# Block-diagonal states, one product per head pair, a flipped Gram copy by DMA, and a newly planned order, in a delta-rule attention with a GELU feed-forward

## The chip, the cores and the metric

The kernel runs on one core of one Trainium2 chip. The metric is the time of the device in microseconds, the median of the runs shown. The engines are named as in the profile: PE (TensorE, with PEld for its weight loads), DVE (VectorE), ACT (ScalarE), POOL (GpSimd) and SP (SyncE, which only issues DMAs here). An engine takes its instructions strictly in the order of its own queue; semaphores join the queues.

## The reference

Batch 4, 8 heads, 768 steps, head size 48; then a feed-forward of 384 by 2048 over 3072 tokens.

```python
k_n = k / (np.linalg.norm(k, axis=-1, keepdims=True) + 1e-06)
for t in range(S):
    y[:, :, t] = np.einsum('bhd,bhde->bhe', q[:, :, t], state)
    v_old = np.einsum('bhde,bhd->bhe', state, kt)
    state = state + bt[:, :, :, None] * np.einsum('bhd,bhe->bhde', kt, vt - v_old)
x = y.transpose(0, 2, 1, 3).reshape(B * S, H * D)
h = x @ w_in
g = 0.5 * h * (1.0 + np.tanh(c * (h + 0.044715 * h * h * h)))
out = g @ w_out
```

## The kernel before

**Tiling.** The 768 steps are cut into 12 chunks of 64. A unit u is one chunk (c = u // 2) of two of the four batches; the two batches (a = 0, 1) lie in the two halves of the 128 partitions, so a unit has 8 heads (g) times 2 batches = 16 small problems, and there are 24 units. Heads are also counted in pairs: head 2h+y, pair h of four, member y. After the transposition (`kT`) the 48 components of member 0 lie from partition 0 on and those of member 1 from partition 64 on, with zero padding between.

**Stages of a unit.** `prep` squares and sums k on ACT or POOL and DVE, takes the square root (L498 on ACT for the first four units, L501 on POOL after that), scales k, multiplies by beta (L506, L508, L512, mostly on POOL), transposes (L519 on PE for units 0 to 7, then L525, a DMA transpose that SP issues), and makes Gram matrices on PE. `gram2` (L543) makes the strictly lower part in 32 products of 64 by 64: x = 0 puts batch a into its own half of the partitions, x = 1 into the other half, the "flipped" copy. One masked copy on DVE (L547) moves all of it into `at`, 128 by 1024. `gram` (L535) makes the upper part and the query part. `newton` then inverts the 16 triangular matrices in five steps of two phases each: `left` (L577) multiplies `lt` with `at`, DVE subtracts the product from 2I (L584), `right` (L591) multiplies again, and ACT or DVE copies the result to `lt`. In steps 1 to 4 `right` puts its result into the other half of the partitions (`hop`), so that steps 2 and 4 read the flipped half of `at`. `chain` carries the states `st` from chunk to chunk: `carried` (L635, k times state), `values` (L648), `smat` (L663, the growth of the state), `queries` (L640) and `omat` (L677). `carried`, `queries` and `smat` are 16 products each, one for each head and batch, on the four 64 by 64 quarters of the array. `mlp_up` (L705) and `mlp` (L722) are the feed-forward, 960 products over the whole array, with the GELU on ACT (L709).

**Order.** Nothing is ordered by hand. `Flow.add` notes each operation with an assumed duration, its inputs and outputs, and a key; `Flow.schedule` runs a model of the engines, and each time that one is free it gives it the ready operation of the lowest key. PE operations carry a mode: "d", "x", "o" and "z" use the 64 by 64 quarters, the others the whole array; changing between the two kinds is charged 0.095 in the model. `BLOCK` and `REFILL` stand for a limit on how fast PE is fed with instructions: 128 matmuls per 3.6 assumed us. PSUM is eight banks, given out by `place`. DMAs are modelled by one `dma_free` time. So every duration that is changed in an `A(...)` call can move everything behind it, on each queue.

**DMAs.** SP issues the loads of k, q, v (L457), the transposes and the stores (L728); POOL issues the six loads of the weights (L469, L472), whose earliest places are set by `W1AT` and `W2AT` through `held`. At the start DVE and ACT clear all of PSUM (L735, L736), and `FILL` operations write identity matrices into `lt` and `at` (L742).

Of the kernel before, what the change touches and what calls it, by code (L numbers as in the profile page):

```python
# [24 lines left out]
class Flow:  # L25
# [9 lines left out]
    DMA_LAT, WLAT, SOFT = 2.6, 4.0, 0.9  # L35
    BLOCK = 128
    REFILL, SLOWFILL, SLOWTIL = 3.6, 5.5, 45.0
# [46 lines left out]
    def schedule(self):  # L84
# [17 lines left out]
        events, t, done, mode, dma_free = [], 0.0, 0, None, 0.0  # L102
# [8 lines left out]
        def room(o):  # L111
            taken, at = set(), {}
            for name, k in sorted(o.alloc, key=lambda x: -x[1]):
                b = place(k, taken)
                if b is None:
                    return None
                at[name] = b
                taken.update(range(b, b + k))
            return at

# [42 lines left out]
        while done < len(self.ops):  # L163
            for e in ENGINES:
                while free[e] <= t + 1e-9:
# [6 lines left out]
                    if o.dma is not None:  # L172
                        issue = self.SOFT if e == "pool" else 0.65
                        dma_free = max(dma_free, t + issue) + d
                        free[e], o.t1 = t + issue, max(dma_free, t + 1.5) + (self.WLAT if o.dma[0] == "w" else self.DMA_LAT)
                        self.queues[e].append(o)
                        heapq.heappush(events, (o.t1, o.seq, o))
                    elif e == "pe":
# [11 lines left out]
                        first = self.BLOCK - self.count % self.BLOCK  # L190
                        for k in range(first, many + 1, self.BLOCK):
                            at = start + extra + long * k / many
                            hold = max(0.0, self.begun + (self.SLOWFILL if at < self.SLOWTIL else self.REFILL) - at)
                            extra += hold
                            self.begun = at + hold
                        self.count += many
# [8 lines left out]
            if not events:  # L205
                raise RuntimeError(f"stuck at {t:.1f}: {done} of {len(self.ops)}")
            t, _, o = heapq.heappop(events)
# [118 lines left out]
def bass_deltanet__then__act_gelu_tanh_kernel(  # L326
# [14 lines left out]
    DP = 112  # L341
# [4 lines left out]
    with nc.allow_non_contiguous_dma("strided loads"), nc.allow_low_precision("bf16 pipeline"):  # L346
# [27 lines left out]
        st = sb("st", [128, 2 * J, D], BF16, 4)  # L374
# [13 lines left out]
        PEO, T1, T2, TX, TX2 = 0.01, 0.0165, 0.029, 0.0105, 0.0185  # L388
        KSTEP, KDN, W1DUR, W2DUR = 0.08, 0.6, 4.6, 2.3
        KUP = [min(4.5, 2.5 + 0.75 * c) for c in range(NC)]  # L390
        LKEY = [-10.0, -9.0, -7.0] + [2 * c - 6.0 for c in range(3, NC)]
        W1AT, W2AT, WKEY, held = [0, 0], [2, 2, 2, 2], 0.0, {}
        CZ, TZ, LAT = 1, 0.296, {2: 1, 3: 2}
# [81 lines left out]
        def prep(u):  # L475
# [62 lines left out]
            def gram2(e, P):  # L538
                for x in range(2):
                    for y, h, a in corners:  # L540
                        r, t = half_rows(y, D), slice(64 * a, 64 * a + 64)
                        c0 = 512 * y + 256 * x + 64 * h
                        yield e.matmul(P(ps("G2"))[half_rows(a ^ x), c0:c0 + 64], kT[s][r, J + h, t], kT[s][r, h, t])  # L543
            A("pe", gram2, 32 * TX + PEO, n=32, reads=[n("kT")], alloc=[(ps("G2"), 2)], mode="x", key=u)
            A("pe", gram, 16 * TX2 + PEO, reads=[n("kT")], alloc=[(ps("G"), 2)], mode="x", key=u)
            wide = lambda m: m.rearrange("p h t -> p (h t)").unsqueeze(1).unsqueeze(1).to_broadcast([128, 2, 2, J * C])
            A("dve", lambda e, P: e.copy_predicated(  # L547
                at[s].rearrange("p x (y h) t -> p y x (h t)", y=2), wide(mlow),
                P(ps("G2")).rearrange("p (y x m) -> p y x m", y=2, x=2)), 1.22,
              reads=MLOW + [f"eye{s}"], frees=[ps("G2")], writes=[n("at")], key=u)  # L550
            g4 = lambda P, x: P(ps("G")).rearrange("p (g x t) -> p x g t", x=2, g=G)[:, x, :, :]
# [8 lines left out]
        def step(u, phase):  # L560
# [4 lines left out]
            qn, hop = n("q5" if i == 5 else "q4" if i == 4 else "qf"), int(i < 5)  # L565
            if phase % 2 == 0:
                pq, f = f"Q{i}.{u}", 1 - i % 2
# [18 lines left out]
                return left, [n("lt"), n("at")] + (ID + TWO if u < UQ else []), pq, "d", take  # L586
            px, lo = f"X{i}.{u}", 0 if hop else 32
# [31 lines left out]
        def chain(u):  # L619
# [12 lines left out]
            def carried(e, P, i):  # L632
                y, h, a = corners[i]
                r = half_rows(y, D)
                return e.matmul(P(ps("R"))[half_rows(a), 512 * y + D * h:512 * y + D * h + D], kT[s][r, J + h, 64 * a:64 * a + 64], so[r, 2 * h + a, :])  # L635

            def queries(e, P, i):
                y, h, a = corners[i]
                r = half_rows(y, D)
                return e.matmul(P(ps("O"))[half_rows(1 - a), 512 * y + D * h:512 * y + D * h + D], kT[s][r, 2 * J + h, 64 * a:64 * a + 64],  # L640
                                so[r, 2 * h + a, :], start=h == 0, stop=False, skip_group_check=True)

            def part(P, name, w, rows=slice(0, 128)):
                return P(name)[rows, :].rearrange("p (y m) -> p y m", y=2)[:, :, 0:J * w].rearrange("p y (h w) -> p y h w", h=J)
# [5 lines left out]
            def each(f):  # L650
                return lambda e, P: (f(e, P, i) for i in range(2 * G))
            if not first:
                A("pe", each(carried), 16 * TX + PEO, reads=[n("kT"), son], alloc=[(ps("R"), 2)], mode="x", key=u - 0.5)
                A("dve", lambda e, P: e.tensor_tensor(rest[:, :, :].rearrange("p (y h) d -> p y h d", y=2),
                                                      vb[s][:, :, :].rearrange("p (y h) d -> p y h d", y=2), part(P, ps("R"), D), ALU.add), 0.55,
                  reads=[n("vb")], frees=[ps("R")], writes=[restn], key=u - 0.5)
            A("pe", each(values), 16 * T1 + PEO, reads=[n("lt"), restn], alloc=[(ps("U"), 1)], mode="d", key=u - 0.5)
# [3 lines left out]
            def smat(e, P):  # L661
                for y, h, a in corners:
                    yield e.matmul(P(ps("S"))[half_rows(y, D), 512 * a + D * h:512 * a + D * h + D], kqb[s][half_rows(a), 0, 2 * h + y, 0:D],  # L663
                                   ub[half_rows(a), J * y + h, :])
            state = lambda ap: ap[0:DP, :, :].rearrange("p (h a) d -> p a h d", a=2)
            if not last:
                A("pe", smat, 16 * TX + PEO, reads=[n("kn"), ubn], alloc=[(ps("S"), 2)], mode="x", key=u - 0.5)
                if first:
                    A(EV, lambda e, P: copy(e, state(sn), part(P, ps("S"), D, slice(0, DP))), ev(384), frees=[ps("S")], writes=[snn], key=u - 0.5)
                else:  # L670
                    A("dve", lambda e, P: e.tensor_tensor(state(sn), part(P, ps("S"), D, slice(0, DP)), state(so), ALU.add), 0.55,
                      reads=[son], frees=[ps("S")], writes=[snn], key=u - 0.5)

            def omat(e, P):
                for g, a in pairs:
                    c0 = 512 * (g // J) + D * (g % J)
                    yield e.matmul(P(ps("O"))[half_rows(1 - a), c0:c0 + D], mnd[s][half_rows(a), g, :], ub[half_rows(a), g, :], start=first and g % J == 0, stop=True, skip_group_check=True)  # L677
            if not first:
                A("pe", each(queries), 16 * TX + PEO, reads=[n("kT"), son, ubn], alloc=[(ps("O"), 2)], mode="x", key=u - 0.41)
            A("pe", omat, 16 * T1 + PEO, reads=[ubn, n("mnd")], alloc=[(ps("O"), 2)] if first else [],  # L680
# [122 lines left out]
```

## Time and profile before

| what | value |
|---|---|
| median of 3 runs (range) | 317.13 us (316.99 to 320.48) |
| the profiled execution: its own time, span | 320.61 us, 318.8 us |
| PE busy, matmuls | 262.5 us (82%), 7920 |
| DVE, ACT, POOL busy | 209.2, 158.4, 126.7 us |
| mean granted clock | 0.957 |
| L705 and L722 on PE (feed-forward) | x576 at 286 ns, x384 at 329 ns |
| L577 and L591 on PE (inversion) | x1920 at 199 ns, x1920 at about 200 ns |
| L543, L663, L635, L640 on PE | x768 at 204 ns, x352 at 189, 198 and 192 ns |
| DMA queues: q1 (SP and ACT), q0 (POOL), q8 (instructions) | 107184, 2912 and 62 packets |

The profiled execution is one run, with its own time; the other runs were 0.1 to 3.6 us shorter. A matmul's duration is from entering the array to leaving it. Many lie in the array at once, so 1920 times 199 ns is not time that anyone waits. What one costs is read from the chain of waits, where each piece stands for what it added. "issue" in that chain is time in which an engine waited for nothing that the profile shows.

### The profile page before, as it was taken

How to read it: one execution, taken by the hardware profiler on the slowest of the kernel's cores; microseconds unless marked ns; L12 is line 12 of the kernel's file. 1: busy time of each engine (PE TensorE's matmuls, PEld its weight loads, DVE VectorE, ACT ScalarE, POOL GpSimd, SP SyncE). 2: the span in 40 equal slices, each digit the busy share in tenths (PEclk: the TensorE clock that was granted, in tenths of full speed). 3: DMA queues.
4: the chain of work that ended last, by engine and by line, in shares of the span. 5: the costliest groups of instructions: out<-in, count | busy, mean ns of one | idle time of the engine just before them, and what ended most of it. 6: DMA issues, size and time to landing. Idle time of an engine off the chain costs nothing.

```text
span 318.8 us, 16988 instructions
## 1 busy us (share of the span) xinstructions
PE 262.5 (82%) x7920; PEld 191.4 (60%) x7920; DVE 209.2 (66%) x387; ACT 158.4 (50%) x285; POOL 126.7 (40%) x156
## 2 busy tenths in 40 slices
PE   0362758899997799689879887989888999999994
PEld 0351747566765576458556566666565766766772
DVE  8872985757798588667948687776466866754100
ACT  5650446553655365426525554455464555655461
POOL 8926475937834563725935429132030000000000
PEclk9999999599998599959979999999999999999999
DMA  8999999898944981690940925427118210112122
GB/s 126 159 191 171 175 179 164 146 160 155 175 68 98 153 155 31 84 145 8 161 88 6 144 60 78 53 67 115 42 26 117 53 29 16 42 29 51 27 51 49
DMA packets 112277, 30.67 MB, mean 96 GB/s; under 512 B 106320, under 2 KB 111440, under 8 KB 112208
## 3 DMA queue, kind: packets, MB, share of 16 engines
q1 hardware_dynamic: 107184, 26.06, 52.9%
q0 software_dynamic: 2912, 3.15, 6.0%
q8 instruction: 62, 1.02, 1.4%
q10 hardware_dynamic: 2112, 0.39, 0.8%
q14 instruction: 7, 0.06, 0.1%
HBM read 20.55 MB, written 4.72 MB: 79 GB/s over the span
## 4 chain that ended last, share of the span: by engine, by line
PE 70%; issue 8%; DVE 7%; POOL 4%; DMA 4%; SPq 4%; ACT 1%; POOLq 0%
PE ps L705 21%; PE ps L722 19%; PE ps L591 8%; PE ps L577 7%; DMA vraw<-in_v_dram 4%; SPq L457 3%; PE ps L677 3%; POOL nrm L501 2%; PE ps L648 2%; PE ps L543 2%; PE ps L519 2%; PE ps L535 2%; PE ps L663 2%; PE ps L635 1%; DVE qf L584 1%
## 5 line engine op out<-in xcount | busy, mean ns | idle before, releaser
L709 ACT ACTIVATE gT<-ps 128x512 bf16<-128x512 f32 x96 | 57.2, 597 | 59.1 <-PE ps L705 56.9
L705 PE MATMUL ps<-xn,W 128*128 128x256 bf16 x576 | 81.8, 286 | 0.3 <-ACT xn L424 0.3
L722 PE MATMUL ps<-W,gT 128*128 128x384 bf16 x384 | 75.0, 329 | 0.0
L424 ACT ACTIVATE lt<-ps 128x512 bf16<-128x512 f32 (+1 forms) x94 | 51.9, 557 | 37.3 <-PE ps L591 19.1
L577 PE MATMUL ps<-at,lt 64*64 64x64 bf16 (+2 forms) x1920 | 55.5, 199 | 8.3 <-issue 4.3
L705 PEld LDWEIGHTS ps<-xn,W 128*128 128x128 bf16 x576 | 53.4, 101 | 12.6 <-ACT xn L424 0.4
L584 DVE TENSOR_TENSOR qf<-ps,two 128x512 bf16<-128x512 f32 x72 | 49.2, 685 | 17.1 <-PE ps L577 9.7
L577 PEld LDWEIGHTS ps<-at,lt 64*64 64x64 bf16 x1920 | 43.7, 116 | 18.8 <-issue 9.6
L501 POOL TENSOR_TENSOR nrm<-nrm,half 128x8 f32<-128x8 f32 x20 | 32.7, 1639 | 30.6 <-DVE nrm L495 30.6
L722 PEld LDWEIGHTS ps<-W,gT 128*128 128x128 bf16 x384 | 33.2, 98 | 18.9 <-issue 0.3
L506 POOL TENSOR_TENSOR kqb<-kraw,nrm 128x384 bf16<-128x384 f32 x24 | 20.0, 835 | 54.2 <-PE ps L663 48.0
L591 PE MATMUL ps<-lt,qf 64*64 64x64 bf16 x1152 | 34.7, 203 | 2.4 <-DVE lt L552 1.3
L584 DVE TENSOR_TENSOR q<-ps,two 128x384 bf16<-128x384 f32 (+1 forms) x48 | 23.3, 486 | 17.3 <-PE ps L591 12.0
L591 PEld LDWEIGHTS ps<-lt,qf 64*64 64x64 bf16 x1152 | 26.4, 115 | 8.9 <-issue 5.3
L424 DVE CAST lt<-ps 128x512 bf16<-128x512 f32 (+1 forms) x26 | 16.0, 618 | 21.6 <-PE ps L577 12.3
L547 DVE CAST_PREDICATED at<-mlow,ps 128x1024 bf16<-128x1024 uint16 x24 | 29.1, 1213 | 1.3 <-PE ps L543 1.1
L512 POOL TENSOR_TENSOR vb<-vraw,bsb 128x384 bf16<-128x384 f32 x24 | 19.8, 833 | 13.0 <-DMA vraw<-in_v_dram 8.1
L591 PE MATMUL ps<-lt,q 64*64 64x64 bf16 (+1 forms) x768 | 22.3, 194 | 0.6 <-DVE q L584 0.5
L591 PEld LDWEIGHTS ps<-lt,q 64*64 64x64 bf16 x768 | 17.4, 115 | 7.1 <-issue 4.5
L424 ACT ACTIVATE ob<-ps 128x384 f32<-128x384 f32 x23 | 11.3, 490 | 16.6 <-PE ps L722 16.3
L519 PE MATMUL ps<-idb,kqb 128*128 128x128 bf16 x96 | 10.2, 285 | 10.4 <-POOL kqb L508 6.1
L543 PE MATMUL ps<-kT 48*64 48x64 bf16 x768 | 12.8, 204 | 7.2 <-issue 3.4
(80 smaller groups left out, 340.1 us busy)
## 6 DMA issues: line engine op xcount, KB each, us to landing
out_dram<-ob SPq DMA_DIRECT2D x48, 96.0 KB, 2.4
kraw<-in_k_dram SPq DMA_DIRECT2D x22, 192.0 KB, 5.3
qraw<-in_q_dram SPq DMA_DIRECT2D x22, 192.0 KB, 5.3
vraw<-in_v_dram SPq DMA_DIRECT2D x22, 192.0 KB, 5.1
W<-in_moe_w_in_dram POOLq DMA_DIRECT2D x2, 768.0 KB, 9.5
W<-in_moe_w_out_dram POOLq DMA_DIRECT2D x4, 384.0 KB, 9.7
qraw<-in_q_dram SPq DMA_DIRECT2D x3, 96.0 KB, 4.5
vraw<-in_v_dram SPq DMA_DIRECT2D x3, 96.0 KB, 4.8
```

The lines of the kernel that those rows point to most:

```text
L424: return e.activation(out, in_, ACT.Copy) if e is nc.scalar else e.tensor_copy(out, in_)
L501: A("pool", lambda e, P: e.tensor_tensor(nr[:, 1, :], nr[:, 0, :], half[:, :], ALU.pow), 1.65, reads=[n("nrm"), "half"], writes=[n("nrm")] ...
L506: A(POOL, lambda e, P: e.tensor_tensor(kq(0), kr, nr[:, 3, :].unsqueeze(2).to_broadcast(full), ALU.mult), tt, reads=[f"kraw{r}", n("nrm")] ...
L512: A(VEC, lambda e, P: e.tensor_tensor(vb[s][:, :, :].rearrange("p (y j) d -> p y j d", y=2), byside(vr), byside(bcol), ALU.mult), tt, read ...
L543: yield e.matmul(P(ps("G2"))[half_rows(a ^ x), c0:c0 + 64], kT[s][r, J + h, t], kT[s][r, h, t])
L547: A("dve", lambda e, P: e.copy_predicated(at[s].rearrange("p x (y h) t -> p y x (h t)", y=2), wide(mlow), P(ps("G2")).rearrange("p (y x m) ...
L577: yield e.matmul(P(pq)[r, C * g:C * g + w], lt[s][r, g, :], at[s][r, f, g, 0:w], start=u >= UQ, stop=True, skip_group_check=True)
L584: A("dve", lambda e, P: e.tensor_tensor(q[:, :, 0:w], bank(P, pq, 0, w), two64[:, 0:w].unsqueeze(1).to_broadcast([128, G, w]), ALU.add), 0 ...
L591: yield e.matmul(P(px)[half_rows(a ^ hop), C * g + lo:C * g + C], q[half_rows(a), g, :], lt[s][half_rows(a), g, lo:C])
L705: yield e.matmul(P(ph)[:, 256 * f:256 * f + 256], W1[:, t, 128 * (i + f):128 * (i + f) + 128], xn_[xi][:, t, :], start=(t == 0), stop=(t = ...
L709: A("act", lambda e, P, i=i, ph=ph: e.activation(gT[gi][:, i:i + 2, :].rearrange("p f t -> p (f t)"), P(ph), ACT.Gelu_apprx_tanh), 0.62, f ...
L722: yield e.matmul(P(po)[:, 0:DM], g_[:, f, 128 * bp:128 * bp + 128], W2[:, f, :], start=(f == 0), stop=(f == FC - 1))
```

## The change

- **Blocks on a diagonal.** The state of a head pair becomes one 128 by 96 tile with member 0 in the upper left and member 1 in the lower right block, and zeros elsewhere, written once at the start by four memsets on POOL. `carried` and `queries` become 8 products each (both members at once, all 128 partitions in, 64 out, 96 columns), `smat` 8 products of 64 in, 128 out, 96 columns. Their modes are now "h" and "w", so they count as whole-array operations. The update of the state takes two operations (one for each member, 64 partitions by 8x48) where there was one (112 by 384). `R` and `O` take one PSUM bank instead of two.
- **Flipped copy by DMA.** `gram2` keeps its first 16 products; the masked copy writes 128 by 512 instead of 128 by 1024; two DMAs per unit, issued by POOL, write the flipped half of `at` from the unflipped one (tile name `af` for the waits). `HOPS` lets steps 2 to 5 hop instead of 1 to 4, so the flipped half is first read in step 3.
- **PSUM is no longer cleared**, and the fill of `at` is half as wide.
- **The planner's model.** DMAs are modelled as one first-in-first-out list for each issuing engine, sharing the bandwidth, and an engine stops issuing when its list is over `BACKLOG`; `BLOCK` is 127.3, `REFILL` 3.8, the weights' assumed durations are smaller, and `W1AT` is [1, 1]. All queues come out in another order.

The instruction counts of the built programs: PE 7008 matmuls where there were 7920 (gram 2: 384 for 768; the three state products: 176 each for 352 each); POOL 163 rows for 142; DVE 397 queue entries for 375, ACT 239 rows for 237; SP's DMAs are the same in kind and number.

```diff
-    DMA_LAT, WLAT, SOFT = 2.6, 4.0, 0.9
-    BLOCK = 128
-    REFILL, SLOWFILL, SLOWTIL = 3.6, 5.5, 45.0
+    DMA_LAT, ISSUE, SOFT, BACKLOG = 2.2, 0.68, 0.9, 7.0
+    BLOCK = 127.3
+    REFILL, SLOWFILL, SLOWTIL = 3.8, 5.0, 45.0
...
+        def flow(until):
+            while True:
+                heads = [x for x in moving.values() if x]
+                if not heads:
+                    break
+                step = min(x[0][1] for x in heads) * len(heads)
...
-                while free[e] <= t + 1e-9:
+                while free[e] <= t + 1e-9 and sum(x[1] for x in moving[e]) < self.BACKLOG:
...
-        st = sb("st", [128, 2 * J, D], BF16, 4)
+        st = sb("st", [128, 2 * J, 2 * D], BF16, 4)
...
-        KSTEP, KDN, W1DUR, W2DUR = 0.08, 0.6, 4.6, 2.3
+        KSTEP, KDN, W1DUR, W2DUR = 0.08, 0.6, 3.2, 1.9
...
-        W1AT, W2AT, WKEY, held = [0, 0], [2, 2, 2, 2], 0.0, {}
-        CZ, TZ, LAT = 1, 0.296, {2: 1, 3: 2}
+        W1AT, W2AT, WKEY, held = [1, 1], [2, 2, 2, 2], 0.0, {}
+        CZ, TZ, LAT, HOPS = 1, 0.296, {2: 1, 3: 2}, (2, 3, 4, 5)
...
             def gram2(e, P):
-                for x in range(2):
-                    for y, h, a in corners:
+                for y, h, a in corners:
...
-                        yield e.matmul(P(ps("G2"))[half_rows(a ^ x), c0:c0 + 64], kT[s][r, J + h, t], kT[s][r, h, t])
+                    yield e.matmul(P(ps("G2"))[half_rows(a), c0:c0 + 64], kT[s][r, J + h, t], kT[s][r, h, t])
...
+            for a in range(2):
+                A("pool", lambda e, P, a=a: e.dma_start(at[s][half_rows(1 - a), 1, :, :], at[s][half_rows(a), 0, :, :]), 0.35, reads=[n("at")],
+                  writes=[n("af")], dma=f"af{s}", key=u)
...
-                pq, f = f"Q{i}.{u}", 1 - i % 2
+                pq, f = f"Q{i}.{u}", sum(x < i for x in HOPS) % 2
...
-                return left, [n("lt"), n("at")] + (ID + TWO if u < UQ else []), pq, "d", take
+                return left, [n("lt"), n("af" if f else "at")] + (ID + TWO if u < UQ else []), pq, "d", take
...
-                y, h, a = corners[i]
-                r = half_rows(y, D)
-                return e.matmul(P(ps("R"))[half_rows(a), 512 * y + D * h:512 * y + D * h + D], kT[s][r, J + h, 64 * a:64 * a + 64], so[r, 2 * h + a, :])
+                h, a = i // 2, i % 2
+                return e.matmul(P(ps("R"))[half_rows(a), 2 * D * h:2 * D * h + 2 * D], kT[s][:, J + h, 64 * a:64 * a + 64], so[:, J * a + h, :])
...
-                for y, h, a in corners:
-                    yield e.matmul(P(ps("S"))[half_rows(y, D), 512 * a + D * h:512 * a + D * h + D], kqb[s][half_rows(a), 0, 2 * h + y, 0:D],
-                                   ub[half_rows(a), J * y + h, :])
+                for h in range(J):
+                    for a in range(2):
+                        yield e.matmul(P(ps("S"))[:, 512 * a + 2 * D * h:512 * a + 2 * D * h + 2 * D], kqb[s][half_rows(a), 0, 2 * h:2 * h + 2, :].rearrange("p y d -> p (y d)"),
+                                       ub[half_rows(a), h::J, :])
...
-        A("dve", lambda e, P: e.memset(P("clr")[:, 0:2048], 0.0), 2.2, alloc=[("clr", NBANK // 2)], frees=["clr"], key=-20)
-        A("act", lambda e, P: e.activation(P("clr2")[:, 0:2048], nrm[NP - 1][:, 1, 0:1].to_broadcast([128, 2048]), ACT.Copy, scale=0.0), 1.9, reads=["warm"],
-          alloc=[("clr2", NBANK // 2)], frees=["clr2"], key=-25)
+        for i in range(4):
+            A("pool", lambda e, P, i=i: e.memset(st[i][:, :, :], 0.0), 0.5, writes=[f"st{i // 2}{i % 2}{y}" for y in range(2)], key=-1.0)
```

## The prediction, made before the changed kernel ran

> **What bounds the kernel now.** The page's last chain comes first, with its DMA queues.
>
> ```profile
> q8 instruction: 62, 1.02, 1.4%
> PE 70%; issue 8%; DVE 7%; POOL 4%; DMA 4%; SPq 4%; ACT 1%; POOLq 0%
> ```
>
> PE carries 70% of the end, and 8% (26 us of 318.8) is "issue", PE standing with nothing to wait for. Queue q8 moves instructions: 62 packets for 7920 matmuls, one for every 128. The next view is the chain of waits from 176 to 200 us, to see where the issue pieces lie.
>
> ```profile
> 181.46 0.82 issue
> ...
> 185.92 0.85 issue
> ...
> 193.45 0.74 issue
> ...
> 197.29 0.95 issue
> ```
>
> They start 4.46, 7.53 (2 x 3.77) and 3.84 us apart. Between the first two PE's timeline holds 14 of L535, 32 of L543, 8 of L722, 6 of L705 and 67 of L577 and L591: 127 matmuls, one packet. So in this stretch PE uses up a packet before the next has come, and a packet takes about 3.8 us, whatever is in it. The table of stretches tells how general that is.
>
> ```profile
> 48.00:64.00 16.00, 13.76 (x353) 10.67 (x353) 9.93 (x20) 9.49 (x16) 12.25 (x16) 0.79 0.94 153
> ...
> 96.00:112.00 16.00, 11.86 (x452) 8.85 (x454) 11.26 (x20) 6.95 (x14) 7.69 (x11) 0.68 0.79 130
> ...
> 176.00:192.00 16.00, 14.33 (x501) 9.91 (x503) 12.18 (x21) 7.82 (x16) 5.12 (x7) 1.00 0.66 101
> ...
> 240.00:256.00 16.00, 14.68 (x509) 10.59 (x508) 11.89 (x20) 7.63 (x15) 0.00 (x0) 1.00 0.44 82
> ```
>
> After the stretch the columns are its length, then PE, PEld, DVE, ACT, POOL, the granted clock, the DMA share and GB/s. From 176 on PE is idle 1.3 to 1.7 us in 16 while it takes some 500 matmuls, four packets. From 78 to 108 us it is otherwise: DVE and POOL stand in the chain there, and the clock falls to 0.68. The start is a third regime, read from the list of waits:
>
> ```profile
> POOL vb L512 <- DMA vraw<-in_v_dram: 8.1, 1, 8.1
> PE ps L519 <- POOL kqb L508: 6.1, 1, 6.1
> ```
>
> The chain and the DMA's own rows have the reason. The v load issued at 13.09 us landed 13.7 us later, where the median of these loads is 4.9; at 13.39 POOL had begun to issue the first weights. POOL stood on that v from 18.8 to 26.8, and PE behind POOL's L508 for 6.1 us.
>
> **Part by part, against this execution (320.6 us, span 318.8).**
>
> *PE's own work.* The chain prices sixteen quarter products of L635, L640 or L663 at 0.13 to 0.24 us; its pieces add to 4.4, 3.8 and 5.0 us, so 13.1/66 = 0.20 us a set. The new sets have 8 products of 96 columns. No row shows that form. L705 does six of 256 columns in 0.65 us, 0.43 ns a column, so 41 ns for 96 and 0.33 a set. L688, with 128 columns and new weights each time, does three in 0.17 us, 57 ns, 0.45 a set; the two halves of a pair side by side would give 0.16. I take 0.33, since L688 shows that a weight load fits: 66 x 0.13 = +8.6 (between -2.6 and +16.5). gram2 loses 16 x 24 = 384 products at 9 ns (0.27 us for 30 at 178.22): -3.5. Changes between quarters and whole array after the first L705 fall from 237 to 215 in PE's queue; in the chain the first pair after one costs 0.14 against 0.03, the first L705 0.76 against 0.65, so 22 x 0.11 = -2.4. Sum +2.7 us.
>
> *Packets.* 912 matmuls fewer are 7.1 packets of 128. In the stretch above, the four packets without their issue pieces are 4.46 - 0.82 = 3.64 us of work, twice (7.53 - 0.85)/2 = 3.34, and 3.84 - 0.74 = 3.10. The same work in 7008/7920 of the instructions makes that 4.11, 3.77 and 3.50 us a packet, and against 3.8 us there lack 0, 2 x 0.03 and 0.30: 0.36 us where it was 2.41, 15%. Of the 26.2 us of issue, 7.4 are four long pieces (1.90 at 104.73, 1.56 at 135.38, 2.48 at 158.71, 1.47 at 222.68), which I leave. The other 18.8 become 2.8: -16.0 us. The ends are 0 (something else is late at the same moments) and -27 (7.1 x 3.8, if every packet were waited for).
>
> The rule that speaks against this term is in the Trainium skill, "Runtime: NRT & Kernel Launch", section "Instruction fetch mechanics": instructions come in blocks of 256, and crossing a block's border is mostly hidden behind dispatch. The block size agrees with q8 (128 matmuls, each with its weight load); "mostly hidden" does not agree with issue pieces of 0.74 to 0.95 us. By the rule this term would be nearly 0 and the whole sum near 0; the row decides.
>
> *Flipped copy.* DVE's L547 (1213 ns) becomes the size of L552 (680 ns): 24 x 0.53 = -12.8 us busy. The second update of the state gives it back: L671 costs 554 ns at 384 elements a row, and 20 more of those are +11.1. DVE is level, so I book nothing; if its cover, PE's chain, were gone, the 0.55 us on each of the 11 steps from state to state would cost 6. ACT gains two pieces of 0.48 and loses L736 (1.86). POOL gains 48 issues. The nearest rows are L472 (772 ns) and L469 (904 ns): 37 to 43 us busy. A unit now costs POOL about 0.83 + 1.64 + 3 x 0.83 + 0.5 = 5.5 us (L493, L501, L506, L508, L512, the q cast), with two issues 7.0, against a pace of 241 us/22 = 11 us a unit: it fits on average. Each pair waits for its masked copy, and behind it in POOL's queue stand the next units' L506, L508 and L512, for which transposes and so PE wait. POOL is last in the chain for 10.5 us after the start; for its busy part (77 to 97 us, two units) I book 2 x 1.54 = +3 (0 to +20). The landing is covered: a store lands in 2.4 us and a load in 5.3 at the median, and step 3 comes four phases after the masked copy, some 6 us at the pace of the timeline (phases at 177.8, 179.2, 181.0, 183.4).
>
> A page prices the issue against it too: the Trainium skill, "SBUF — State Buffer", section "A bandwidth-pool intuition that's wrong (but worth ruling out)", has DMAs from the GpSimd queue starve while certain DVE copies hold a shared port, 620 ns becoming 3100. By that all 48 issues would cost up to 119 us more on POOL; L469's issue at 13.39 us, beside DVE's L508 and L742, took 1.01 us against 0.80 for the next: a little of it, not five times.
>
> *Start.* In POOL's new queue the first weight issue comes behind both units' scaling, about 3 us later than 13.39, so the v load lands near 18, and the 6.1 us of PE go. Against it: four memsets twice as wide as L745 (429 ns) stand before `ident`, 1.7 to 3.4 us; the wait for PSUM's clearing (L735, 1.76) and 1.4 of POOL's at fill go. The flipped copy of unit 0 stands behind the first weights in POOL's queue and that of unit 2 behind all four loads of W2; the six took 6.7 to 13.0 us to land. I book -3 (-8 to +6).
>
> *New order.* R and O free a bank each, and all queues are dealt anew. DVE and POOL are last for some 26 us between 59 and 300; no row says how much of it another order keeps. Bound: half of it either way, 13; taken -3, the side of the two banks that come free.
>
> Sum: +2.7 - 16.0 + 3 - 3 - 3 = -16.3 us, 304.3 in this execution. That one ran 3.5 us above the median of the runs; 317.1 - 16.3 = 301.
>
> **Rivals.** (1) PE gets its instructions, but waits: the packets' -16 is eaten by waits for POOL or DVE in the same places. For it speaks 78 to 108 us, where PE is not last; against it, that from 176 on PE is idle almost only for issue. It gives the sum without most or all of that term: 312 to 320. (2) Slower: POOL becomes the bound. Place: the pair of issues, waiting for its masked copy with the next units' scaling queued behind. It begins once a pair stands longer than 11 - 7.0 = 4 us and outweighs the -16 over some 20 units at 4.8; at 5.5 us each POOL needs 12.5 us a unit, 1.5 x 20 = +30, less 16: 331. Against it: POOL's stretches hold 12.25 of 16 us at most. (3) More: every packet taken away is 3.8 us, and the start gains its 6: -27 + 2.7 - 6 + 3 = -27.3, so 290. (4) That the change does less than it says is excluded for the counts: the built program has 7008 matmuls.
>
> **How the numbers follow.** About 2%, 6.3 us, is what a measurement of this kernel tells from no change. Forecast 0.56 (its own range 293 to 312, of which 0.04 above 310.8), rival 1 0.16, rival 2 0.16, rival 3 0.12. Faster 0.52 + 0.12 = 0.64, same 0.20, slower 0.16. The range takes in rivals 1 and most of 3 and leaves out 2 and the far end of 3: 285 to 320.
>
> **What would show it.** Right: PE's matmuls 7008 and q8 near 55 packets; issue in the chain near 10 us; the rows of the three state products near 0.33 us a set in the chain; no 8 us wait of POOL on v; L547's successor near 680 ns; flipped copies landing within 6 us. Wrong: "POOL" waiting for DVE in front of the new DMAs and PE waiting for kT or for the flipped copy; issue pieces as many as before.

## The result, and the profile after

| | before | changed kernel |
|---|---|---|
| median (range) | 317.92 us (316.99 to 320.48, 4 runs) | 302.80 us (301.07 to 303.84, 4 runs) |
| profiled execution, span | 320.61 us, 318.8 us | 302.04 us, 300.2 us |
| mean granted clock there | 0.957 | 0.993 |
| ratio of the times, 95% interval | | 0.951 (0.943 to 0.959) |

The changed kernel is faster by 4.9%, 15.1 us by the medians; 301 was predicted. Ratios, here and below, leave out executions more than 1.5% above the fastest of their kernel, so that a ratio can differ from the quotient of the medians shown, and the stages of such an execution are not read. The clock is not what does it: the changed kernel's four runs had mean clocks from 0.943 to 0.993 and lay within 2.8 us, and among the experiments below the one with 912 products added back had 0.989 and took 321.78 us, the one with the flip issued by SP had 0.920 and the shortest middle.

In the changed kernel's code L607 and L621 are `left` and `right`, L571 `gram2`, L564 `gram`, L574 the masked copy, L579 the flipping DMAs, L664, L668 and L692 `carried`, `queries` and `smat`, L703 the update of the state, L737 and L754 the feed-forward, L548 the transposition and L541 beta times v.

From the page of the changed kernel: the instruction queue, the shares of the last chain, and the groups that the change made or altered (in a group: busy us, mean ns of one, idle time before them and its releaser).

```profile
span 300.2 us, 15241 instructions
PE 255.4 (85%) x7008; PEld 185.5 (62%) x7008; DVE 208.5 (69%) x408; ACT 158.3 (53%) x290; POOL 150.8 (50%) x202
...
q8 instruction: 55, 0.90, 1.4%
...
PE 76%; DVE 10%; issue 6%; DMA 3%; ACT 3%; SPq 1%
...
L579 POOL DMA_DIRECT2D at<-at x48 | 26.3, 551 | 50.5 <-DVE at L574 45.6
...
L703 DVE TENSOR_TENSOR st<-ps,st 64x384 bf16<-64x384 f32 x40 | 22.0, 551 | 2.5 <-PE ps L692 1.8
...
L574 DVE CAST_PREDICATED at<-mlow,ps 128x512 bf16<-128x512 uint16 x24 | 16.4, 681 | 6.0 <-PE ps L571 5.9
```

55 packets carry the 7008 matmuls. PE's share of the end rises from 70 to 76%, issue falls from 8 to 6%, and POOL, 4% before, is gone from the chain, although it is busy 24 us longer. Its 45.6 us of standing in front of the flipping DMAs are large and cost nothing that the chain shows.

The same four stretches as before (length, PE, PEld, DVE, ACT, POOL with instructions, granted clock, DMA share, GB/s), then the issue pieces of the chain between 176 and 200 us:

```profile
48.00:64.00 16.00, 13.85 (x296) 10.88 (x293) 11.09 (x23) 10.19 (x17) 12.08 (x16) 1.00 0.98 163
96.00:112.00 16.00, 12.99 (x322) 8.99 (x321) 11.43 (x22) 6.95 (x13) 9.38 (x13) 0.89 1.03 177
176.00:192.00 16.00, 13.19 (x470) 9.25 (x463) 12.89 (x27) 7.60 (x15) 9.91 (x11) 1.00 0.42 73
240.00:256.00 16.00, 16.00 (x427) 11.32 (x426) 11.04 (x20) 9.36 (x18) 2.08 (x4) 1.00 0.25 56
```

```profile
178.33 1.44 issue
...
183.37 0.36 issue
...
187.02 0.60 issue
...
195.26 0.05 issue
```

In the last stretch PE took 509 matmuls in 16 us and stood 1.3 us; it now takes 427 and never stands. In the third it stands longer than before (2.8 us for 1.7). Between 176 and 200 us the issue pieces are 2.45 us, where four of 0.74 to 0.95 were 3.36. They are shorter and not gone: a packet that holds little work, like that before 187.02 (3.65 us after the one before it), is still waited for.

That these stalls belong to packets can be counted in the traces. Take every idle stretch of PE's weight loads above 0.45 us that is put down to issue, from the first to the last: in both kernels they lie 127 or 128 weight loads apart, or a multiple of some 127.3. One does not fit, 0.94 us at 61.2 in the changed kernel. The four long pieces that the prediction left out of its packet term (at 104.73, 135.38, 158.71 and 222.68) do fit.

For the balance I cut the span at the first feed-forward product (58.4 us; before, 59.1) and 19 us before the end, where only feed-forward is left and both kernels do the same. Sums of the chain's pieces by engine:

| us | span of it | PE | issue | DVE | POOL | DMA | ACT |
|---|---|---|---|---|---|---|---|
| middle, before | 240.6 | 190.3 | 22.7 | 16.1 | 11.0 | 0 | 0.4 |
| middle, changed | 222.9 | 187.2 | 10.0 | 16.7 | 0 | 4.9 | 4.1 |
| middle, changed, run again | 222.7 | 176.9 | 8.1 | 29.9 | 0 | 5.1 | 2.7 |

So the time came out of the middle (-17.7), and by the chain out of issue (-12.7), POOL (-11.0) and PE's own work (-3.1). Transposes of x (4.9) and ACT (+3.7) took some of it. The start gave 0.8 us. Two limits: the profiled execution of before was 2.7 us above its median and that of the changed kernel 0.8 below, so these differences add to more than the 15.1 us; and the last row, the same program in another execution, keeps the length of the middle but moves some 10 us between PE and DVE. In this pair the lengths agree closely and the shares of the chain only roughly.

The lines of the start show why it gave so little. First the chain's issue pieces there, then the list of waits, then the flipping DMAs up to 50 us and after it:

```profile
32.95 1.36 issue
...
39.00 2.06 issue
...
44.56 2.97 issue
```

```profile
POOL vb L541 <- DMA vraw<-in_v_dram: 7.7, 1, 7.7
...
PE ps L548 <- DVE kqb L537: 6.8, 1, 6.8
```

```profile
L579 POOL DMA_DIRECT2D at<-at x8: 524/565/602, 18.6 to 42.5; - x8
...
DMA to landing us min/median/max: 4.1/6.3/13.2
```

```profile
L579 POOL DMA_DIRECT2D at<-at x40: 524/524/597, 57.9 to 252.8; - x40
...
DMA to landing us min/median/max: 1.9/2.6/4.8
```

PE's wait of 6.1 us for POOL and v at 24 us is gone: the v load that landed at 26.79 now lands at 18.62, and the third set of transpositions starts at 24.39 instead of 30.23. But three issue stalls of 6.4 us in sum follow, where before there were two, of 0.49 at 42 and 1.35 at 46.6. They end at 34.31, 41.06 and 47.53, 6.7 and 6.5 us apart, and between the first two PE's timeline holds 128 matmuls, one packet. In this stretch (20 to 50 us) the 16 DMA engines are busy throughout (nine tenths or more in every slice of the page) with both sets of weights, k, q, v and the flipped copies. So a packet that takes 3.8 us elsewhere takes 6.7 here. The 6.8 us in the list are another wait, for unit 0's scaling before 14.40 (before, 4.3 us until 13.92). The v wait of 7.7 us is one of a later load, from 33.4 to 41.2, beside PE's stalls.

### The profile page after: what moved, and what is told of

The parts are those of the page before. It is cut to its first block, busy times and chain, and to the rows that moved or that the text cites. A ratio compares the mean times of both kernels' runs of the same rounds, so it can differ in the third digit from the quotient of the medians.

```text
span 300.2 us, 15241 instructions
## 1 busy us (share of the span) xinstructions
PE 255.4 (85%) x7008; PEld 185.5 (62%) x7008; DVE 208.5 (69%) x408; ACT 158.3 (53%) x290; POOL 150.8 (50%) x202
## 3 DMA queue, kind: packets, MB, share of 16 engines
q0 software_dynamic: 4448, 6.29, 10.8%
## 4 chain that ended last, share of the span: by engine, by line
PE 76%; DVE 10%; issue 6%; DMA 3%; ACT 3%; SPq 1%
PE ps L737 22%; PE ps L754 22%; PE ps L621 9%; PE ps L607 8%; PE ps L548 2%; DVE st L703 2%; PE ps L676 2%; PE ps L564 2%; PE ps L692 2%; DVE qf L614 2%; DMA qraw<-in_q_dram 2%; DMA xn<-xo 2%; PE ps L571 2%; PE ps L709 2%; PE ps L668 1%
## 5 line engine op out<-in xcount | busy, mean ns | idle before, releaser
L741 ACT ACTIVATE gT<-ps 128x512 bf16<-128x512 f32 x96 | 57.1, 597 | 49.9 <-PE ps L737 47.4
L737 PE MATMUL ps<-xn,W 128*128 128x256 bf16 x576 | 76.4, 276 | 1.7 <-DMA xn<-xo 1.4
L754 PE MATMUL ps<-W,gT 128*128 128x384 bf16 x384 | 76.1, 328 | 1.3 <-issue 1.3
L453 ACT ACTIVATE lt<-ps 128x512 bf16<-128x512 f32 x82 | 48.5, 595 | 35.6 <-PE ps L621 22.4
L737 PEld LDWEIGHTS ps<-xn,W 128*128 128x128 bf16 x576 | 52.9, 99 | 13.5 <-DMA xn<-xo 1.8
L607 PE MATMUL ps<-at,lt 64*64 64x64 bf16 (+2 forms) x1920 | 52.3, 196 | 7.7 <-issue 4.4
L607 PEld LDWEIGHTS ps<-at,lt 64*64 64x64 bf16 x1920 | 41.4, 113 | 17.5 <-issue 9.8
L579 POOL DMA_DIRECT2D at<-at x48 | 26.3, 551 | 50.5 <-DVE at L574 45.6
L754 PEld LDWEIGHTS ps<-W,gT 128*128 128x128 bf16 x384 | 32.6, 98 | 19.4 <-issue 1.3
L453 DVE CAST lt<-ps 128x512 bf16<-128x512 f32 x38 | 26.2, 688 | 15.9 <-PE ps L607 10.4
L621 PE MATMUL ps<-lt,qf 64*64 64x64 bf16 x1152 | 33.2, 201 | 1.3 <-DVE qf L614 0.8
L621 PEld LDWEIGHTS ps<-lt,qf 64*64 64x64 bf16 x1152 | 25.6, 114 | 7.9 <-issue 4.4
L541 POOL TENSOR_TENSOR vb<-vraw,bsb 128x384 bf16<-128x384 f32 x24 | 20.0, 837 | 11.5 <-DMA vraw<-in_v_dram 7.7
L621 PE MATMUL ps<-lt,q 64*64 64x64 bf16 x768 | 22.6, 199 | 3.1 <-issue 2.1
L703 DVE TENSOR_TENSOR st<-ps,st 64x384 bf16<-64x384 f32 x40 | 22.0, 551 | 2.5 <-PE ps L692 1.8
L621 PEld LDWEIGHTS ps<-lt,q 64*64 64x64 bf16 x768 | 17.0, 111 | 8.2 <-issue 4.9
L574 DVE CAST_PREDICATED at<-mlow,ps 128x512 bf16<-128x512 uint16 x24 | 16.4, 681 | 6.0 <-PE ps L571 5.9
L537 POOL TENSOR_TENSOR kqb<-kqb,bsb 128x384 bf16<-128x384 bf16 x23 | 19.0, 829 | 0.6
```

The costliest lines, as they stand in the source:

```text
L453: return e.activation(out, in_, ACT.Copy) if e is nc.scalar else e.tensor_copy(out, in_)
L541: A(VEC, lambda e, P: e.tensor_tensor(vb[s][:, :, :].rearrange("p (y j) d -> p y j d", y=2), byside(vr), byside(bcol), ALU.mult), tt, read ...
L579: A("pool", lambda e, P, a=a: e.dma_start(at[s][half_rows(1 - a), 1, :, :], at[s][half_rows(a), 0, :, :]), 0.35, reads=[n("at")], writes=[ ...
L607: yield e.matmul(P(pq)[r, C * g:C * g + w], lt[s][r, g, :], at[s][r, f, g, 0:w], start=u >= UQ, stop=True, skip_group_check=True)
L621: yield e.matmul(P(px)[half_rows(a ^ hop), C * g + lo:C * g + C], q[half_rows(a), g, :], lt[s][half_rows(a), g, lo:C])
L703: A("dve", lambda e, P, diag=diag, made=made: e.tensor_tensor(diag(sn), made(P), diag(so), ALU.add), 0.55, reads=[f"{son}{y}"], frees=[ps( ...
```

## The experiments

The theory after the result: the gain in the middle is the number of PE's instructions, since PE waits for packets, and the new order by itself gives nothing there; the order pays only in the start. Rivals: the new order made the gain; or PE's shorter work (gram 2, the state products) made it; or POOL's disappearance from the chain. "Middle" is the span between the same two cuts as above. Ratios are to the kernel before in the same group of runs (medians 315.74, 316.58 and 316.40); the changed kernel, run again with the second group, had 299.71 us (297.81 to 302.43), ratio 0.948 (0.938 to 0.958), first feed-forward product at 57.1, middle 222.7.

| kernel | matmuls, packets | median us | ratio (95%) | first product at | middle |
|---|---|---|---|---|---|
| planner's model alone | 7920, 62 | 317.59 | 1.013 (1.004 to 1.022) | 59.0 | 238.3 |
| blocks, no flip by DMA | 7392, 58 | 304.66 | 0.972 (0.964 to 0.980) | 54.4 | 229.0 |
| flip by DMA, old states | 7536, 59 | 310.50 | 0.988 (0.979 to 0.996) | 57.1 | 230.5 |
| 912 narrow products added | 7920, 62 | 321.78 | 1.027 (1.019 to 1.034) | 60.7 | 239.1 |
| 24 long products added | 7032, 55 | 307.35 | 0.975 (0.967 to 0.982) | 56.5 | 230.1 |
| old planner's model | 7008, 55 | 311.73 | 0.985 (0.975 to 0.996) | 68.4 | 223.0 |
| second weights much later | 7008, 55 | 306.81 | 0.973 (0.964 to 0.982) | 60.7 | 224.0 |
| second weights a little later | 7008, 55 | 306.47 | 0.962 (0.951 to 0.974) | | |
| flip issued by SP | 7008, 55 | 313.03 | 0.988 (0.983 to 0.992) | 73.2 | 219.8 |
| flip issued by ACT | 7008, 55 | 306.86 | 0.968 (0.959 to 0.977) | 53.1 | 230.2 |
| PSUM cleared again | 7008, 55 | 303.25 | 0.960 (0.953 to 0.968) | 55.5 | 224.5 |

**The planner's model alone.** The kernel before, its computation and its clearing kept, with the new `Flow`, `W1DUR`, `W2DUR` and `W1AT`:

```diff
-    BLOCK = 128
-    REFILL, SLOWFILL, SLOWTIL = 3.6, 5.5, 45.0
+    BLOCK = 127.3
+    REFILL, SLOWFILL, SLOWTIL = 3.8, 5.0, 45.0
...
-        W1AT, W2AT, WKEY, held = [0, 0], [2, 2, 2, 2], 0.0, {}
+        W1AT, W2AT, WKEY, held = [1, 1], [2, 2, 2, 2], 0.0, {}
```

> The planner's new model alone: states, flipped Gram half, PSUM clearing and so all 7920 matmuls as in the kernel before, in a new order. Theory 1 (instruction packets): the 62 packets stay, so issue in the chain after the first feed-forward product stays near 22 us and the time is 312 to 318 us. Rival (order: POOL and DVE off the chain is what paid): 303 to 307 us, issue whatever it was.

Ratio 1.013. The time is inside the expected 312 to 318 us, but issue was expected to stay near 22. In its chain's middle POOL falls from 11.0 to 3.3 us and issue from 22.7 to 16.6, and yet the time stays: PE has 193.7 (+3.4), DMA 5.0 and DVE 18.3 in their places. So with the old computation a new order moves shares between labels and gains nothing, and "POOL left the chain" is no cause by itself.

**Each half of the change alone.** The changed kernel with the flipped half made by PE again, and the changed kernel with the old states, which also has the two PSUM banks for `R` and `O` and the clearing of before:

```diff
-                for y, h, a in corners:
+                for x in range(2):
+                    for y, h, a in corners:
...
-            for a in range(2):
-                A("pool", lambda e, P, a=a: e.dma_start(at[s][half_rows(1 - a), 1, :, :], at[s][half_rows(a), 0, :, :]), 0.35, reads=[n("at")],
```

> The changed kernel with the flipped half made on PE again (32 products in gram2, masked copy of 1024, no DMA from POOL): 7392 matmuls, the block states stay. Theory 1: 528 of the 912 matmuls are saved, so 4.1 of the 7.1 packets: 307 to 311 us. Rival (order): as the changed kernel, 301 to 305. If the DMA on POOL costs anything, this one is below 307.

```diff
-        st = sb("st", [128, 2 * J, 2 * D], BF16, 4)
+        st = sb("st", [128, 2 * J, D], BF16, 4)
...
-                A("pe", each(carried, G), G * TH + PEO, n=G, reads=[n("kT"), son + "0", son + "1"], alloc=[(ps("R"), 1)], mode="h", key=u - 0.5)
+                A("pe", each(carried), 16 * TX + PEO, reads=[n("kT"), son], alloc=[(ps("R"), 2)], mode="x", key=u - 0.5)
```

> The changed kernel with the old states (16 products a set, one update of 112 by 384, two PSUM banks for R and O, PSUM cleared): 7536 matmuls, the flipped copy by DMA stays. Theory 1: 384 matmuls or 3.0 packets saved, 309 to 313 us. Rival (order): 301 to 305. If the whole-array products of the block states cost PE the 8.6 us that were booked, this one gains that back and lies at 302 to 306 although it has more packets.

Against the model alone, the blocks take 528 matmuls and 9.3 us from the middle (17.6 ns each), the flip 384 and 7.8 (20.3 ns), both together 912 and 15.4 (16.9 ns). These are differences of single profiled executions. A packet of 128 at 3.8 us would be 29.7 ns a matmul. By the ratios, 0.972/1.013 times 0.988/1.013 is 0.935; 0.951 and 0.948 over 1.013 are 0.938 and 0.935. So both halves pay, nearly additively, in proportion to the instructions that they save, though what they save on PE, DVE and POOL is quite different. Two things do not fit so well. The blocks alone were expected at 307 to 311 us and had 304.66, in the range of the rival: their middle lies where theory put it, but their start is 4.0 us shorter than the changed kernel's (2.7 when that is run again), so the flip's DMAs may cost something there. And with the flip alone the chain's issue in the middle is 20.0 us for 59 packets, against 16.6 for the 62 of the model alone and 11.1 for the 58 of the blocks: from run to run it is the length of the middle that follows the count, not the label issue.

**Instructions given back.** The changed kernel in its own order, with 912 extra products of 8 columns into parts of PSUM that the next products overwrite; then a control with little more than the time, 24 products of 512 columns over the whole array.

```diff
+                    if h == 3 or h == 2 and y != a:
+                        e.matmul(P(ps("G"))[half_rows(a), 512 * y + 128 * h:512 * y + 128 * h + 8], kT[s][r, h, t], kT[s][r, J + h, 64 * a:64 * a + 8])
...
+                    for _ in range(2):
+                        e.matmul(P(ps("G2"))[half_rows(a), c0:c0 + 8], kT[s][r, J + h, t], kT[s][r, h, 64 * a:64 * a + 8])
                     yield e.matmul(P(ps("G2"))[half_rows(a), c0:c0 + 64], kT[s][r, J + h, t], kT[s][r, h, t])
```

> The changed kernel in its own order (the planner is not told), with 912 narrow products of 8 columns added to the two Gram steps, each overwritten by the product behind it: 7920 matmuls again, the packets of the kernel before. They cost PE's array about 912 x 9 ns = 8 us. Theory 1: issue in the chain after the first feed-forward product goes from 10 to 20 us or more and the time to 314 to 322 us. Rival (order): only the array's 8 us or less, 303 to 311 us, issue as in the changed kernel.

```diff
             def gram2(e, P):
+                e.matmul(P(ps("G2"))[:, 0:512], idb[:, :], kT[s][:, 0:4, :].rearrange("p x t -> p (x t)"))
```

> The changed kernel in its own order with one long product (whole array, 512 columns, overwritten by what follows) at the head of each gram2: 24 products more, some 24 x (0.22 + 0.22 for the two changes between quarters and whole array) = 10.5 us of work for PE, but only 0.2 packets. Control for the 912 narrow products, which made 321.8 us with 9.9 us more of PE in the chain. If PE's work alone is what counts: 312 to 316 us, and the rest of the 19 us there, 6 to 9, was the packets. If the packets play no part, this one comes to 318 to 322 as well.

The pages of the two, packets and chain, first with the narrow and then with the long products:

```profile
q8 instruction: 62, 1.02, 1.3%
...
PE 75%; DVE 11%; issue 8%; POOL 2%; ACT 2%; DMA 1%; POOLq 0%
```

```profile
q8 instruction: 55, 0.90, 1.3%
...
PE 74%; DVE 12%; issue 6%; ACT 3%; DMA 2%; POOL 1%; POOLq 0%
```

With 7920 matmuls again the time is 321.78 us, the gain is gone. The control is no perfect one; it came to 307.35, below the 312 to 316 that were expected of PE's work alone. Both Gram lines together take 9.6 us more of the chain in the first kernel (20.4 for 10.8), and 2.8 more in the second (13.6); the spans are 18.6 and 5.4 us longer. That leaves 9.0 and 2.6 us beside PE's own work, and 6.4 between them for 888 instructions, 6.9 packets: 0.9 us a packet. The idle stretches at packet borders agree: those above 0.35 us add to 18.2 us in the middle with the narrow products, to 11.3 with the long ones, and to 10.8 and 7.9 in the two executions of the changed kernel, which is 1.0 to 1.5 us a packet. So extra instructions cost more than their time in the array, and they cost it at the packet borders, which is shown; but this measures a smaller price than the removal does. The middle's issue rose only from 10.0 to 16.4 us, not to the expected 20 or more, and the control's is 14.1 with almost no more instructions, so the chain's "issue" is uncertain by some 4 us.

**The planner's model undone.** The changed kernel with both edits and the old `Flow`:

```diff
-        KSTEP, KDN, W1DUR, W2DUR = 0.08, 0.6, 3.2, 1.9
+        KSTEP, KDN, W1DUR, W2DUR = 0.08, 0.6, 4.6, 2.3
...
-        W1AT, W2AT, WKEY, held = [1, 1], [2, 2, 2, 2], 0.0, {}
+        W1AT, W2AT, WKEY, held = [0, 0], [2, 2, 2, 2], 0.0, {}
```

> Both edits of the computation with the planner's old model (one dma_free time, BLOCK 128, REFILL 3.6, W1AT 0). 7008 matmuls. Theory 1 (packets): most of the gain stays, 302 to 308 us. Rival (order): the gain goes, 314 to 318. Since the new model alone gave 317.6 us, the new model may still matter here, where it knows of two DMAs per unit that the old one puts into one line with the loads: up to 5 us.

The time fell between the two ranges expected (302 to 308 and 314 to 318). The middle is 223.0 us, that of the changed kernel (222.9 and 222.7), in another order; the whole loss of 10 to 11 us is in the start. Its chain names it: the first weights are issued at 12.21, and the v load behind that lands 14.5 us after its issue.

```profile
12.98 14.54 DMA vraw<-in_v_dram
```

So the new model is worth about 10 us to the new computation and nothing to the old one, whose start was already at 59 us.

**The second weights later.** `W2AT` at [4, 4, 5, 5], and at [3, 3, 4, 4]:

```diff
-        W1AT, W2AT, WKEY, held = [1, 1], [2, 2, 2, 2], 0.0, {}
+        W1AT, W2AT, WKEY, held = [1, 1], [4, 4, 5, 5], 0.0, {}
```

> The changed kernel with W2AT [4, 4, 5, 5] in place of [2, 2, 2, 2]: the loads of W2 leave later. In the changed kernel PE's packets came every 6.7 us between 21 and 48 us, against 3.8 later. If that is the load on the DMA engines by W2's large pieces, the packets between 27 and 41 us come every 4 to 5.5 us, the flipped copy of unit 2 lands in under 7 us (11 and 12.6 before), and the time is 298 to 302. If the small pieces of the k, q, v loads do it, nothing changes: 301 to 304. If W2 is then late for its first product, PE waits there: 303 to 307.

> The second weights are taken from phase 3 and 4 on (W2AT [3,3,4,4]) instead of 2, between the changed kernel (2) and the run with 4 and 5. Theory: the flipped copy of unit 2 lands in under 6 us and the packets in the start come every 4 to 6 us instead of 6.7; whether this pays depends on the order that follows, so the gain, if any, is 1 to 4 us in the start (first feed-forward product at 54 to 58 us), rest near 223 to 226: ratio 0.935 to 0.96. Rival (the start is set by the order of DVE and POOL, not by the weights): first product at 58 to 61 us, ratio 0.955 to 0.98.

With the first, PE waits for a packet until 32.71 and, two packets on, until 41.61: 8.9 us for two, where the changed kernel has 6.7 and 6.5 for one. The next comes 6.6 us later, at 48.16, behind second weights issued at 39.98 and 40.81. Unit 2's flipped copies land 3.5 and 4.7 us after their issue instead of 11.7 and 13.2. So it was the weights that held up both. It doesn't pay, though 298 to 302 us were expected: the stalls move with the weights (2.13 us at 46, 2.74 at 57; issue in the start's chain is 7.8 us for 7.6), the order made around it has 24.1 us of DVE in the start's chain (12.1 in the changed kernel; 16.7 when run again), and the first feed-forward product comes at 60.7. The granted clock in its profile was 0.62 from 32.7 to 41.6 and 0.50 from 48.2 to 59.8, where the changed kernel had 1.00 from 20 to 50; what that adds is not separated. The second run lies between; its interval touches that of the changed kernel, and nothing is settled by it.

**Who issues the flipping DMAs.** SP, then ACT, in place of POOL:

```diff
-                A("pool", lambda e, P, a=a: e.dma_start(at[s][half_rows(1 - a), 1, :, :], at[s][half_rows(a), 0, :, :]), 0.35, reads=[n("at")],
+                A("sp", lambda e, P, a=a: e.dma_start(at[s][half_rows(1 - a), 1, :, :], at[s][half_rows(a), 0, :, :]), 0.35, reads=[n("at")],
```

> The 48 flipping DMAs are issued by SP instead of POOL, all else as in the changed kernel; the order is planned anew (PE 7008 matmuls, q8 55 packets). Theory: POOL's 26 us of issuing and its 45.6 us of waiting for the masked copy cost nothing after the first feed-forward product, so the rest of the span stays near 223 us (between 220 and 227); what can gain is the start, where the flipped copies of units 0 and 2 (5.6 and 11 to 12.6 us) no longer stand behind the weights in POOL's queue: they should land within 4 us. Time 0.93 to 0.955 of the kernel before. Rival (the pair standing in POOL's queue is a hidden cost): the rest falls by 5 us or more, and the ratio under 0.93. Third way: SP's list, with loads, transposes and stores, becomes the one that stands still, and x transposes or k loads come later: ratio 0.96 to 0.98.

> The 48 flipping DMAs are issued by ACT, which does the GELU and copies of the inversion. If a DMA issue that waits for its masked copy blocks what is queued behind it, this must be worse than SP: ACT is busy 158 us of 300 with work that PE waits for, and the POOL version shows about 1.9 us of waiting for the masked copy per unit. Theory: ratio 0.955 to 0.99, with ACT taking over 8 us of the chain after the first feed-forward product (4.1 in the changed kernel). Rival (waiting issues are free, since the planner puts them where the copy is done): ratio 0.94 to 0.955.

With SP the middle is 219.8 us, 3 less than in the changed kernel, so POOL's 26 us of issuing and its long waits cost it little. The start loses 15 us, and the chain of that run, with one line of PE's timeline (start, length, and idle time before it with its releaser), shows on what:

```profile
18.25 3.85 SPq L486
...
22.14 6.45 SPq L486
...
28.63 14.36 DMA vraw<-in_v_dram
```

```profile
43.59 0.48 PE L607 MATMUL ps<-at,lt 64*64 64x64 bf16 x10 [5.32 <-DMA at<-at]
```

L486 is the loading of k, q and v. In SP's queue the first two flipping DMAs stand behind q and v loads whose issues take 3.85, 6.45 and 4.93 us each among the weights: they go out at 33.60 and 37.92, where POOL issued them at 18.55 and 19.10. PE then stands 5.32 us for a flipped copy, and the next transpositions come at 44.73, after a v that landed at 42.98 and for which POOL stood. So the third way of the expectation came, by more than it said: the list that stands still is SP's, only what it holds back is the flip more than the loads. With ACT I expected ACT to become late. It did not: ACT has 2.2 us of the middle, but DMA 24.0 (nearly all of it transposes of k), POOL 15.0 and SP's queue 8.8, with the first product as early as 53.1. The ratio is inside the range expected, for another reason. Why that order leaves the transposes late stays open. It shows that 55 packets alone do not make a short middle: an order can cost 7 us of it.

**Clearing put back.** The changed kernel with the two clearing operations of before:

```diff
+        A("dve", lambda e, P: e.memset(P("clr")[:, 0:2048], 0.0), 2.2, alloc=[("clr", NBANK // 2)], frees=["clr"], key=-20)
+        A("act", lambda e, P: e.activation(P("clr2")[:, 0:2048], nrm[NP - 1][:, 1, 0:1].to_broadcast([128, 2048]), ACT.Copy, scale=0.0), 1.9, reads=["warm"],
```

> The two operations that clear PSUM are put back into the changed kernel (2048 columns each on DVE and ACT, about 1.8 us each in the trace of before), all else kept; the order is planned anew, 7008 matmuls. Theory: clearing stands beside the first loads and costs at most 2 us in the start; ratio 0.945 to 0.965. Rival: it delays the first transposes by its whole 1.8 us and, through the other order, the start by more than 5 us: ratio over 0.965. The same ratio as the changed kernel within 0.005 would mean that this part of the change gives nothing by itself.

303.25 us, ratio 0.960 (0.953 to 0.968) beside 0.951 (0.943 to 0.959): the intervals overlap, and its start is not longer (55.5 us). So no gain from leaving out the clearing is shown; the intervals leave room for some 2%.

None of these kernels beats the changed one. Not tested apart is what the freed PSUM banks give, which go with the blocks.

## Why the prediction was right, point by point

The likeliest case came, and at nearly its time: 302.8 against 301, well inside its own range of 293 to 312. Its terms were less good than their sum, and that the sum came within 2 us is in part luck: packets and start gave less than was booked, PE's own work and POOL came out better.

- **Packets, -16.0.** The right mechanism: the stalls lie at packet borders, and products added in the same order bring them back. The size is not confirmed. The middle's issue fell by 12.7, but the planner's model alone, with all 62 packets, took 6.1 of that (22.7 to 16.6) and no time with it. From there to the changed kernel it is 6.6, or 0.9 us a packet, which is also the price of the added products. Removal priced by time is 16.9 ns a matmul, or 2.2 us a packet, near the 2.25 of -16.0 for 7.1 packets; but that takes in PE's own pieces, which fell from 193.7 to 187.2. Nothing came near 3.8, so rival 3 was rightly small. Issue over the whole span fell from 26.2 to 17.6 us (-8.6), not to 10, because the start's rose by 4.2. The prediction was also wrong to set the four long pieces apart: they are packet borders like the rest. The Trainium skill, "Runtime: NRT & Kernel Launch", section "Instruction fetch mechanics", has block crossings mostly hidden. The 0.9 us that each added packet cost beyond its products' own time speak against it for this kernel.
- **PE's own work, +2.7.** It was -3.1 in the middle, as far as the chain's shares can be trusted. The step that failed is +8.6 for the state sets: the prediction set a full price of 0.33 us against a mean of 0.20 that counts the sets lying beside other work. The like sums are 13.8/66 = 0.21 us a set and 0.20, so the term was +0.7 (run again, 11.6/66 = 0.18, -1.5). For a set that stands whole in the chain 0.33 was not far off: a set of 8 costs 0.28 to 0.29 us in most rows, where whole sets of 16 cost 0.10 to 0.41 us, 0.19 at the mean, so a whole set did become dearer. The rows show such a set of 8:

```profile
276.44 0.29 PE ps L668 x8
```

- **gram 2**, -3.5: -0.9 in the chain (4.9 for 5.8). Before, only 449 pieces of the chain belonged to its 768 products; the rest lay beside other work.
- **POOL, +3.** The wrong sign: POOL left the chain (-11.0). The issue costs 551 ns, not the 772 to 904 of the weights' issues, hence 26.3 us busy, not 37 to 43; and POOL stands in front of L579 where nothing waits behind it. Rival 2 needed more than 4 us a unit, and the mean is 45.6/24 = 1.9. But the planner's model alone took 7.7 of those 11.0 out of the chain without a gain, so POOL's sign is no proof of a gain by POOL. The Trainium skill, "SBUF — State Buffer", section "A bandwidth-pool intuition that's wrong (but worth ruling out)", has DMAs from the GpSimd queue wait while certain DVE copies hold a shared port. It shows nowhere in these issues: 524 to 602 ns for all 48.
- **Landing within 6 us.** Right after 50 us (2.6 at the median, 4.8 at most), wrong before (13.2 at most), for the reason that was named: unit 2's stands behind the second weights.
- **Start, -3.** The v load landed at 18.6 as predicted and the 6.1 us went; 0.8 came out. In the chain of the start the waits for loads went from 25.4 us (DMA 13.7, SP's queue 11.7) to 7.5, and in their place stand PE with 25.3 for 16.9, DVE with 12.1 for 6.2 and issue with 7.6 for 3.4, the last from packets that come late under the weights. The prediction had the 3.8 us of a quiet stretch for every stretch. "No 8 us wait of POOL on v" was wrong too: there is one of 7.7, for a later load, and it cost nothing that the chain shows.
- **DVE level.** +0.6 in the middle; L574 takes 681 ns as said, L703 551.
- **New order, -3.** The order alone is worth nothing in the middle (238.3 for 240.6, 223.0 for 222.9) and 10 us in the start of the changed kernel. It can also cost: the order with ACT as the issuer has a middle of 230.2. What was booked as one number is really a condition: without the new model the same edits would have given 1.5%, not 5%.

## What to carry to other kernels

Where the chain of waits shows short pieces of issue at even distances on PE, count its instructions, not its columns: one 96-column product for two of 48 paid although a set that stands whole in the chain became dearer, and a flipped copy by DMA paid although it put 26 us on POOL. Before pricing a set of products from the chain, separate those that stand alone in it from those that lie between others. And when a change of order lets one load come earlier, look for what else uses the DMA engines in that stretch, the instruction packets among them.

## What was not expected of the hardware

- A packet of PE's instructions takes 3.8 us in a stretch with DMA shares of 0.42 to 0.66, and 6.5 to 6.7 us while the weights are loading; with the second weights moved away two came in 8.9.
- A DMA of 64 KB from one half of the partitions to the other takes POOL 524 to 602 ns to issue and lands after 2.6 us at the median, but after 11.7 and 13.2 us behind four weight loads of 384 KB in the same queue.
